# An attention and MLP kernel: the Sync queue's order where the bias table ends, and six tiles' low parts and scalings given to GpSimd in the last attention unit

## The chip, the cores and the metric

One core of one Trainium2 chip. The engines are TensorE (PE; its weight loads are shown as PEld), VectorE (DVE), ScalarE (ACT), GpSimd (POOL) and SyncE (SP), which in this kernel only issues DMAs. The metric is the device time of one execution in microseconds, the lower the better.

## The reference, cut to what matters

```python
B, H, S, D = 4, 8, 576, 64              # hidden of the bias MLP: 32
scores = scale * q @ k.T                 # per batch and head, 576 x 576
x = log1p(|i - j|) / log1p(max(i, 1))    # relative position
bias = relu(x * w1 + b1) @ w2            # one 576 x 576 table per head
attn = softmax(scores + bias)            # with 1e-9 in the divisor
out = attn @ v                           # -> x: 2304 tokens x 512
...
h = x @ w_in                             # 512 -> 2048
g = where(h >= 1, h, where(h <= -1, 0, (h + 1)**2 / 4))
y = g @ w_out                            # 2048 -> 512
```

## The kernel before, in words

The kernel has three stages that overlap at their seams.

**The bias table.** 36 groups `G` of 16 rows of the position table are worked out for all eight heads (ACT and POOL make masks `u`, PE sums them, DVE combines to a tile `y`). Each group's `y` goes to a buffer in HBM by one DMA on the Sync queue (line 332). There are five buffers `bias_d[0..4]`: groups 0 to 7 fill the first, 8 to 15 the second, 16 to 23 the third, 24 to 31 the fourth, and 32 to 35 the last one.

**Attention.** 16 units `n`, one for each of four head pairs `p` and four batches `b` (`n = 4p + b`). In a unit, `k` runs over four blocks of 128 query rows for both heads (`j` = 0, 1) and a fifth block `k = 4` that holds the 64 left rows of both heads (names with `_L`). `scores` (lines 466, 467; 487, 488) makes the scores in PSUM tiles `S` of which there are two, DVE adds the bias and takes the maximum (469, 489), and ACT takes the exponential (476, 495). `transposes` and `shared` (532, 537, 546) bring the result into PSUM tiles `T`, which share four places with the outputs `O` of `values` (570, 572). `split` takes a `T` apart into a high part `hi` and a low part `lo = T - hi`, which PE reads as float32r. There are two ways: either ACT copies `hi` out of PSUM (507) and DVE subtracts (508), or ACT copies the tile to `c` in SBUF (512), POOL (514) or DVE (516) makes `hi`, and POOL subtracts (517). The function `EV` takes the second way for the five blocks `(k, j)` of `POOL` in units 0 to 14, and the first way throughout in unit 15. In the setting `hi='pvvpv'` the blocks (0,1) and (3,0) have their `hi` by POOL and (2,0), (2,1), (3,1) by DVE.

`load_bias(p, k)` brings the bias of one head pair and block to SBUF: three DMAs on the Sync queue for `k < 4` (443 to 445), two for `k = 4` (449). The first pair's five loads are traced ahead of the loop over units, those of pair `p + 1` at fixed places `LB` in the units of pair `p`. `prep(n)` loads a unit's q, k and v; its `part` copies the low and high parts of k to the other half of the partitions by two DMAs on the Sync queue (206, 207).

**The MLP.** `x` (the attention output, stored to HBM as `xT`, line 625) is loaded in quarters `(k, j)` by `split_x` (388, 397), scaled by `scaled` (404: an addition and a multiplication, each 128x384), and taken apart by `high` on ACT (411) and `rest` on POOL (418). The first 768 tokens' eight quarters are loaded and prepared during the attention, at steps given in `XQ`: step `10n + i` is the `i`-th of ten steps of unit `n`, so that the quarter (2,1) is scaled at unit 15's step 1 and (3,1) at its step 5. Weights come in as int64 and are unpacked by `weight` (109, 114 to 119), those of the first two blocks during the attention. The first raw tile of `wout` of the MLP's loop uses the buffer that the quarter (3,1) leaves.

**What sets the order.** The program is traced in the order of the code, and a list scheduler then orders each engine's instructions by readiness and trace order. `keep` (`keep_in_program_order`) pins an instruction behind the one traced before it on its engine. `pool` does so for POOL while `go[0]` is set, which is from the first unit to the start of unit 15. `tc.issue_after(ins)` queues the instructions of its block behind `ins` on the same engine, without a wait for its end. An engine, and the Sync queue too, works through its instructions strictly in order: one that waits holds up all behind it.

```python
for k in range(5):
    e, later = scores(n, k, qkv[n], bias[p])
    ...
    step(2 * k)          # jobs of step 10n + 2k, then the bias loads of LB
    ...
    drain(...)           # transposes and values that lag behind
    exp_()
    step(2 * k + 1)
```

Of the kernel before, what the change touches and what calls it, by code (L numbers as in the profile page):

```python
# [18 lines left out]
B, H, S, D = 4, 8, 576, 64  # L19
# [13 lines left out]
EPS = 1e-9  # L33
RB = 2
LASTP = CFG["lastp"]
XQ = {(0, 0): (39, "raw", 43), (1, 0): (79, "raw", 83), (2, 0): (118, "raw", 123), (3, 0): (137, "bias", 142),
      (0, 1): (125, "x", 136), (1, 1): (131, "raw", 145), (2, 1): (139, "x", 151), (3, 1): (148, "raw", 155)}
WQ = {(0, 0): (49, 53), (0, 1): (59, 63), (1, 0): (89, 93), (1, 1): (99, 103)}
# [9 lines left out]
def attn_cpb_moe_kernel(ctx, tc, qk, vL, cb, win, wout, lw, ident, ii, out):  # L48
    nc = tc.nc
# [26 lines left out]
    ac = loads.enter_context(tc.tile_pool(name="a_const", side="right", bufs=1))  # L76

    qa = [ac.tile([P, 2, QW], F32R, name=f"qa{i}") for i in range(2)]
    wi, wo, last_y = [], [], []
    half_s = wp0.tile([P, 1], F32, name="half_s")  # L80
    nc.gpsimd.memset(half_s, 0.5)
    eps_s = wp0.tile([P, 1], F32, name="eps_s")
# [69 lines left out]
    go = [False]  # L152
# [7 lines left out]
    def keep(ins):  # L160
        tc.keep_in_program_order(ins)

    def pool(ins):
        if KEEP and go[0]:
            tc.keep_in_program_order(ins)
# [53 lines left out]
    with ExitStack() as ph:  # L219
# [101 lines left out]
        def combine(G, A, Bp):  # L321
            right, left, n_ = span(G)
            t = tp.tile([P, S], F32, tag="t", name=f"t{G}")
            y = tp.tile([P, S + 15], F32, tag="y", name=f"y{G}")
            nc.vector.scalar_tensor_tensor(out=t[:, :n_], in0=A[:, :n_], scalar=sg_s[:, G : G + 1], in1=lw8[:, :n_], op0=ALU.mult, op1=ALU.mult)
            for o, c in ((y[:, :left], slice(left, 0, -1)), (y[:, left : left + right], slice(0, right))):
                last_y.append(nc.vector.scalar_tensor_tensor(out=o, in0=Bp[:, c], scalar=s8, in1=t[:, c], op0=ALU.mult, op1=ALU.add))

            r0 = 16 * (G % 8) * H * BW + 1
            dst = bias_d[G // 8][r0 : r0 + 16 * (H * BW + 1)].rearrange("(i w) -> i w", i=16)[:, : H * BW]  # L330
            dst = dst.rearrange("i (h w) -> i h w", h=H)[:, :, : S + 15]
            nc.sync.dma_start(out=dst, in_=y)

        prev = None
        for G in range(NG):
# [38 lines left out]
    def split_x(blk, k, j, home=None):  # L374

        src = xT[k][blk // TB][:, :, TH * j : TH * j + TH].rearrange("(s d) i c -> d s i c", s=2)
        rp, n_ = x_pool() if home is None else (rps[0], home != "raw")
        if n_:
            if home == "bias":
                r = bp.tile([P, 2 * S], F32, tag="bias", name=f"x{blk}_{k}_{j}").rearrange("p (a b) -> p a b", a=3)  # L380
            else:
                r = rp.tile([P, 3, TH], F32, tag="x", name=f"x{blk}_{k}_{j}", bufs=n_)
            r, rr = r[:, 0:2], r[:, 2]
        else:
            r = rp.tile([P, 2 * DM], F32, tag="raw", name=f"x{blk}_{k}_{j}")[:, : 2 * TH].rearrange("p (a b) -> p a b", a=2)
            rr = rp.tile([P, DM], F32, tag="a", name=f"xr{blk}_{k}_{j}")[:, :TH]
        for i in range(2):
            nc.sync.dma_start(out=r[D * i : D * i + D], in_=src[:, :, i])
        c0 = blk + TH * j
        c1 = c0  # L390
        while c1 < c0 + TH:
            t = c1 % S
            e = min(c0 + TH, c1 - t + (512 if t < 512 else S))
            for i in range(2):
                at = 512 * i + t if t < 512 else 1024 + D * i + t - 512
                row = rT[k][c1 // S][at : at + e - c1].unsqueeze(0)
                nc.sync.dma_start(out=rr[D * i : D * i + D, c1 - c0 : e - c0], in_=row.to_broadcast((D, e - c1)))
            c1 = e

        x = r[:, 0]  # L400

        def scaled():
            for op, in1 in ((ALU.add, r[:, 1]), (ALU.mult, rr)):
                a = nc.vector.tensor_tensor(out=x, in0=x, in1=in1, op=op)
                if home:
                    keep(a)

        def high():
            z = (2 * (blk // TB) + j) % 3
            xs[blk, k, j] = [x_tile(z, k, i, f"x{'hl'[i]}{blk}_{k}_{j}") for i in range(2)]  # L410
            a = nc.scalar.copy(xs[blk, k, j][0], x)
            if home:
                keep(a)

        def rest():
            h, l = xs[blk, k, j]
            if home:
                pool(nc.gpsimd.tensor_tensor(out=l, in0=x, in1=h.bitcast(F32), op=ALU.subtract))
            else:
                nc.vector.tensor_tensor(out=l, in0=x, in1=h.bitcast(F32), op=ALU.subtract)  # L420

        if home:
            return scaled, high, rest
        scaled()
        high()
        rest()

    with ExitStack() as ph:
# [8 lines left out]
        def load_bias(p, k):  # L437
            if k < 4:
                if (p, k) in ((1, 1), (2, 3)):
                    t = rps[0].tile([P, 3, TH], F32, tag="x", name=f"bias{p}_{k}", bufs=1).rearrange("p a b -> p (a b)")  # L440
                else:
                    t = bp.tile([P, 2 * S], F32, tag="bias", name=f"bias{p}_{k}")
                nc.sync.dma_start(out=t[:, 0:S], in_=bias_r[k][:, 2 * p, :])
                nc.sync.dma_start(out=t[:, S : S + D], in_=bias_r[k][:, 2 * p + 1, 512:S])
                nc.sync.dma_start(out=t[:, S + D : 2 * S], in_=bias_r[k][:, 2 * p + 1, 0:512])
            else:
                t = bp.tile([P, S], F32, tag="biasL", name=f"biasL{p}", bufs=2)
                for j in range(2):
                    nc.sync.dma_start(out=t[D * j : D * j + D, :], in_=bias_r[4][:, 2 * p + j, :])
            return t  # L450

        def scores(n, k, qkv, bias):
# [65 lines left out]
                pool(r)  # L518

        def EV(n, k, j):  # L520
            return nc.gpsimd if (k, j) in POOL and n < LASTP else None

        def transposes(n, k, es, eT):
            hi, lo = eT
# [55 lines left out]
                c1 = e  # L580

        N = NP * B
        bias = {0: [load_bias(0, k) for k in range(5)]}
        es, eT, sums = {}, {}, {}
        queue, late = [], []

# [51 lines left out]
        for n in range(N):  # L638
            p, b = n // B, n % B
            if n + 2 < N:  # L640
                preps[n + 2] = prep(n + 2)
            es[n] = []
            if n >= LASTP:
                go[0] = False
            for k in range(5):
                e, later = scores(n, k, qkv[n], bias[p])
                es[n].append(e)
                exps = [False]

                def exp_():  # L650
                    if not exps[0]:
                        exps[0] = True
                        for f in later:
                            exps.append(f())

                if CFG["ex"][k] == 0:
                    exp_()
                step(2 * k)
                if p + 1 < NP:
                    for k_ in range(5):  # L660
                        if (b, k) == LB[k_]:
                            bias.setdefault(p + 1, {})[k_] = load_bias(p + 1, k_)

                def tr(n=n, k=k):
                    half = k // 2 if k < 4 else 1
                    if k in (0, 2):
                        w = 256 + D * half
                        eT[n, half] = (
                            (tp0, tp1)[half].tile([P, 9, w], F32R, tag=f"hi{half}", name=f"hi{n}_{half}"),
                            (tp0, tp1)[half].tile([P, 9, w], F32R, tag=f"lo{half}", name=f"lo{n}_{half}"),  # L670
                        )
                    transposes(n, k, es[n], eT[n, half])
                    if k in (1, 4):
                        shared(n, half, es[n], eT[n, half])

                def inv(n=n):
                    nc.vector.reciprocal(out=sums[n], in_=sums[n])

                def rc(n=n):
                    recips(n)  # L680

                if k in (1, 4):
                    def av(n=n, half=0 if k == 1 else 1):
                        values(n, half, es[n], eT[n, half], qkv[n]["v"])
                    queue.append([tr, inv] if k == 4 else [tr])
                    late.append([CFG["lag"][0 if k == 1 else 1], [av] if k == 1 else [av, rc]])
                else:
                    queue.append([tr])
                while late and late[0][0] <= 0:
                    queue.append(late.pop(0)[1])  # L690
                for x in late:
                    x[0] -= 1
                drain(CFG["dr"][k], exp_, CFG["ex"][k])
                exp_()
                step(2 * k + 1)
        queue += [x for _, x in late]
        while queue:
            drain(len(queue) - 1)
# [163 lines left out]
```

## Time and profile before

| | |
|---|---|
| three runs | 756.10, 756.09 and 757.43 us, median 756.1 |
| the profiled execution | 759.95 us, of which the span from the first to the last instruction is 758.2 us |
| PE busy | 712.8 us (94% of the span), mean granted clock 0.993 |
| PEld, DVE, ACT, POOL busy | 631.5, 457.0, 471.6, 414.1 us |

The profiled execution is 3.85 us above the median of the runs. Times in rows are microseconds from the start of the span unless a column says ns. The bias table runs to about 70 us, the attention from there to about 350, the MLP to the end.

### The profile page before, as it was taken

The page shows a single profiled execution, that of the slowest core. Times are in us where ns is not written, and L with a number is a line of the kernel's source. Part 1 is how long each engine was busy: PE and PEld are TensorE (multiplying, and loading weights), DVE is VectorE, ACT ScalarE, POOL GpSimd, SP SyncE. Part 2 cuts the span into 40 slices and gives each one's busy share as a digit, 9 for nine tenths or more (in the row PEclk, how much of TensorE's full clock was granted, in tenths as well). Part 3 has the DMA queues.
Part 4 walks back from the last instruction along what each step waited for, and adds up shares of the span by engine and source line. Part 5 has one row for each costly group of instructions (what it writes and reads, how often), then busy time and mean ns, then how long its engine had stood idle before and what let it go on. Part 6 is the DMA issues. An engine that isn't in the chain of part 4 may idle for free.

```text
span 758.2 us, 13397 instructions
## 1 busy us (share of the span) xinstructions
PE 712.8 (94%) x4688; PEld 631.5 (83%) x4688; DVE 457.0 (60%) x921; ACT 471.6 (62%) x1037; POOL 414.1 (55%) x352
## 2 busy tenths in 40 slices
PE   5777899999999999998999999999999999999997
PEld 2224899998888889988988889898999999999996
DVE  6889778988898898885555642653222252222222
ACT  7997799888888889878997533432222333222222
POOL 8885587888888887853987432222222222222221
PEclk9999999999999999999999999999999999999999
DMA  8889887987997897635575520550000021000002
GB/s 217 249 257 262 223 200 201 272 237 188 262 220 208 199 257 197 168 95 199 194 222 164 157 73 1 149 149 26 1 1 1 0 74 42 0 1 1 1 0 84
DMA packets 58515, 103.35 MB, mean 136 GB/s; under 512 B 12480, under 2 KB 32464, under 8 KB 58448
## 3 DMA queue, kind: packets, MB, share of 16 engines
q1 hardware_dynamic: 56000, 92.44, 42.7%
q0 software_dynamic: 2304, 9.96, 6.5%
q8 instruction: 37, 0.61, 0.3%
q14 instruction: 30, 0.25, 0.1%
q10 hardware_dynamic: 144, 0.09, 0.0%
HBM read 67.38 MB, written 25.12 MB: 122 GB/s over the span
## 4 chain that ended last, share of the span: by engine, by line
PE 63%; DMA 9%; DVE 6%; ACT 6%; issue 4%; POOL 3%; SPq 0%; DVEq 0%; ACTq 0%; POOLq 0%
PE y L743 7%; PE y L744 7%; PE y L742 7%; PE h L721 7%; PE h L723 7%; PE h L722 7%; PE O L570 7%; PE T L532 4%; PE S L466 3%; PE S L467 3%; DMA x<-xT 2%; DMA bias_d<-y 2%; DMA xT<-x 2%; PE O L572 2%; DMA rawo<-in_wout_dram 2%
## 5 line engine op out<-in xcount | busy, mean ns | idle before, releaser
L734 POOL TENSOR_TENSOR gl<-c,gh 128x384 fp32r<-128x384 f32 x96 | 99.9, 1040 | 259.5 <-ACT gh L733 236.3
L731 ACT ACTIVATE c<-c,half_s 128x384 f32<-128x384 f32 x96 | 59.1, 615 | 168.3 <-DVE c L730 168.1
L730 DVE TENSOR_SCALAR c<-h 128x384 f32<-128x384 f32 x96 | 53.2, 555 | 142.2 <-PE h L723 142.2
L721 PE MATMUL h<-xh,wi 128*128 128x384 f32 x352 | 119.7, 340 | 1.8 <-DVE c L732 1.7
L517 POOL TENSOR_TENSOR lo<-c,hi 128x512 fp32r<-128x512 f32 x75 | 101.2, 1365 | 33.9 <-DVE hi L516 31.4
L723 PE MATMUL h<-xh,wi 128*128 128x384 f32 x352 | 118.7, 337 | 0.0
L722 PE MATMUL h<-xl,wi 128*128 128x384 f32 x352 | 118.2, 336 | 0.0
L744 PE MATMUL y<-wo,gl 128*128 128x512 f32 x288 | 114.0, 396 | 0.0
L743 PE MATMUL y<-wo,gh 128*128 128x512 f32 x288 | 113.7, 395 | 0.0
L742 PE MATMUL y<-wo,gh 128*128 128x512 f32 x288 | 111.9, 389 | 0.0
L476 ACT ACTIVATE e<-e,mx 128x576 f32<-128x576 f32 x128 | 100.6, 790 | 11.7 <-DVE mx L469 11.5
L469 DVE CUSTOM_DVE_ANT_0 e<-S,bias 128x576 f32<-128x576 f32 x128 | 94.6, 750 | 15.5 <-PE S L467 12.4
L466 PE MATMUL S<-kh,qa 128*128 128x288 f32 x256 | 78.9, 324 | 9.6 <-DVE mx L469 5.7
L732 DVE TENSOR_TENSOR c<-h,c 128x384 f32<-128x384 f32 x96 | 53.4, 556 | 53.7 <-ACT c L731 53.7
L733 ACT CAST gh<-c 128x384 fp32r<-128x384 f32 x96 | 49.2, 512 | 50.3 <-DVE c L732 48.4
L721 PEld LDWEIGHTS h<-xh,wi 128*128 128x128 f32 x352 | 66.1, 188 | 9.0 <-DVE c L732 5.0
L532 PE MATMUL T<-id_s,e 128*128 128x128 f32 x512 | 71.1, 275 | 2.0 <-DVE hi L516 1.0
L467 PE MATMUL S<-ls,qa 128*128 128x288 f32 x256 | 72.4, 301 | 0.0
L722 PEld LDWEIGHTS h<-xl,wi 128*128 128x128 f32 x352 | 66.1, 188 | 2.5
L723 PEld LDWEIGHTS h<-xh,wi 128*128 128x128 f32 x352 | 66.0, 188 | 0.0
L744 PEld LDWEIGHTS y<-wo,gl 128*128 128x128 f32 x288 | 54.0, 187 | 11.5
L532 PEld LDWEIGHTS T<-id_s,e 128*128 128x128 f32 x512 | 59.2, 142 | 4.6 <-DVE lo L508 1.3
(117 smaller groups left out, 1523.0 us busy)
## 6 DMA issues: line engine op xcount, KB each, us to landing
bias_d<-y SPq DMA_DIRECT2D x36, 295.5 KB, 5.2
qk<-in_qk_dram SPq DMA_DIRECT2D x16, 608.0 KB, 4.5
qa<-in_qk_dram POOLq DMA_DIRECT2D x16, 608.0 KB, 7.2
x<-xT SPq DMA_DIRECT2D x48, 192.0 KB, 3.7
rawo<-in_wout_dram SPq DMA_DIRECT2D x14, 512.0 KB, 3.2
rawi<-in_win_dram SPq DMA_DIRECT2D x14, 512.0 KB, 4.6
v<-in_vL_dram SPq DMA_DIRECT2D x16, 320.0 KB, 3.0
qa<-ls SPq DMA_DIRECT2D x32, 152.0 KB, 5.3
```

The source lines that it names most:

```text
L466: nc.tensor.matmul(ps[:, hf, :HS], qs[:, qc], kh[:, kc : kc + HS], start=True, stop=False)
L467: nc.tensor.matmul(ps[:, hf, :HS], q0[:, qc], kl[:, kc : kc + HS], start=False, stop=True)
L476: lambda ev=ev, j=j: nc.scalar.activation(ev, ev, AF.Exp, bias=mx[:, j : j + 1], scale=-1.0, accum_out=sm[:, 4 * j + k : 4 * j + k + 1])
L517: r = nc.gpsimd.tensor_tensor(out=lo, in0=m, in1=hi.bitcast(F32), op=ALU.subtract)
L532: nc.tensor.transpose(ps[:, tb, :], e[:, c0 : c0 + P], id_s)
L721: nc.tensor.matmul(ps[:, :TH], wh_, xh, start=k == 0, stop=False)
L722: nc.tensor.matmul(ps[:, :TH], wh_, xl, start=False, stop=False)
L723: nc.tensor.matmul(ps[:, :TH], wl_, xh, start=False, stop=k == NK - 1)
L734: nc.gpsimd.tensor_tensor(out=gl, in0=c, in1=gh.bitcast(F32), op=ALU.subtract)
L742: nc.tensor.matmul(y, gh[:, c], wo[f][0], start=f == 0, stop=False)
L743: nc.tensor.matmul(y, gh[:, c], wo[f][1], start=False, stop=False)
L744: nc.tensor.matmul(y, gl[:, c], wo[f][0], start=False, stop=f == NF - 1)
```

## The change

1. The first pair's loads: blocks 0 to 2 stay ahead of the loop; block 3's three DMAs are queued behind the last of the 36 stores of `y`; block 4's two DMAs are traced only at unit 0's block 3.
2. The second pair's bias loads (`p == 1`) are pinned to their traced place on the Sync queue. Those of pairs 0, 2 and 3 are not.
3. In unit 15, the blocks (0,1), (2,0), (2,1) and (3,0) are taken apart by the second way, with the low part by POOL; (3,1) stays with ACT and DVE.
4. The quarters (2,1) and (3,1) of the first 768 tokens are scaled by POOL in place of DVE, pinned in POOL's order.
5. `go[0]` is cleared behind the loop in place of at unit 15's start, so that POOL's instructions in unit 15's steps are pinned too.

```diff
+LATE = ((0, 1), (2, 0), (2, 1), (3, 0))
+XP = ((2, 1), (3, 1))
...
-            nc.sync.dma_start(out=dst, in_=y)
+            stored.append(nc.sync.dma_start(out=dst, in_=y))
...
             for op, in1 in ((ALU.add, r[:, 1]), (ALU.mult, rr)):
+                if home and (k, j) in XP:
+                    pool(nc.gpsimd.tensor_tensor(out=x, in0=x, in1=in1, op=op))
+                    continue
                 a = nc.vector.tensor_tensor(out=x, in0=x, in1=in1, op=op)
...
+            for o, i in parts:
+                x = nc.sync.dma_start(out=o, in_=i)
+                if p == 1:
+                    keep(x)
             return t
...
-            return nc.gpsimd if (k, j) in POOL and n < LASTP else None
+            return nc.gpsimd if (k, j) in POOL and (n < LASTP or (k, j) in LATE) else None
...
-        bias = {0: [load_bias(0, k) for k in range(5)]}
+        bias = {0: {k: load_bias(0, k) for k in range(3)}}
+        with tc.issue_after(stored[-1].ins):
+            bias[0][3] = load_bias(0, 3)
...
-            if n >= LASTP:
-                go[0] = False
             for k in range(5):
+                if (n, k) == (0, 3):
+                    bias[0][4] = load_bias(0, 4)
                 e, later = scores(n, k, qkv[n], bias[p])
...
+        go[0] = False
         queue += [x for _, x in late]
```

## Rows read from the trace of the kernel before

**Rows 1.** The page's first part: busy time, share of the span, instructions.

```profile
PE 712.8 (94%) x4688; PEld 631.5 (83%) x4688; DVE 457.0 (60%) x921; ACT 471.6 (62%) x1037; POOL 414.1 (55%) x352
```

**Rows 2.** Windows at the first seam: length, engines' busy time, clock, DMA share, GB/s.

```profile
66.70:71.60 4.90, 2.84 (x40) 2.08 (x39) 4.90 (x11) 1.90 (x3) 1.76 (x2) 1.00 1.05 251
71.60:75.00 3.40, 2.37 (x17) 2.02 (x17) 3.19 (x8) 2.22 (x6) 1.17 (x1) 1.00 0.84 252
75.00:80.00 5.00, 4.96 (x39) 4.55 (x38) 2.49 (x7) 4.76 (x12) 1.91 (x2) 1.00 0.91 254
80.00:83.00 3.00, 0.96 (x4) 0.99 (x5) 2.31 (x6) 1.17 (x3) 0.00 (x0) 0.86 0.19 48
```

**Rows 3.** Timeline of the Sync queue, first seam: start, time to issue, line, DMA.

```profile
71.63 0.33 SPq L443 DMA_DIRECT2D bias<-bias_d  x1
...
74.04 0.59 SPq L445 DMA_DIRECT2D bias<-bias_d  x1
...
75.31 0.61 SPq L332 DMA_DIRECT2D bias_d<-y  x1
75.96 2.37 SPq L207 DMA_DIRECT2D kh<-kh  x1
...
81.61 1.11 SPq L449 DMA_DIRECT2D biasL<-bias_d  x2
```

**Rows 4.** Waits of the Sync queue from 55 to 90: total, times, longest.

```profile
SPq L443 <- DMA bias_d<-y: 7.1, 3, 4.8
```

**Rows 5.** Timeline of DVE, first seam; in brackets the idle time before.

```profile
80.69 0.76 DVE L469 CUSTOM_DVE_ANT_0 e<-S,bias 128x576 f32<-128x576 f32 x1 [2.56 <-PE S_L L488]
...
85.51 0.76 DVE L489 CUSTOM_DVE_ANT_0 e_L<-S_L,biasL 128x576 f32<-128x576 f32 x1 [1.92 <-DMA biasL<-bias_d]
```

**Rows 6.** Timeline of PE, first seam.

```profile
82.04 0.46 PE L466 MATMUL S<-kh,qa 128*128 128x288 f32 x1 [2.08 <-DMA kh<-kh]
...
91.92 0.63 PE L532 MATMUL T<-id_s,e 128*128 128x128 f32 x4 [1.01 <-DVE hi L516]
```

**Rows 7.** Windows after PE's two long gaps, and the middle of unit 15.

```profile
82.00:86.00 4.00, 3.96 (x20) 3.98 (x21) 2.08 (x5) 1.35 (x3) 1.27 (x1) 0.57 0.68 187
331.10:335.00 3.90, 3.90 (x16) 3.90 (x17) 2.77 (x7) 2.77 (x8) 1.20 (x2) 0.56 0.29 79
332.30:343.00 10.70, 10.70 (x80) 10.64 (x79) 7.91 (x18) 8.15 (x21) 1.01 (x1) 0.88 0.34 89
```

**Rows 8.** Timeline of PE: the longest gap within the attention's steady part.

```profile
216.17 0.41 PE L466 MATMUL S<-kh,qa 128*128 128x288 f32 x1 [1.55 <-DVE mx L469]
```

**Rows 9.** Timeline of DVE around unit 15's start.

```profile
326.58 1.36 DVE L404 TENSOR_TENSOR x<-x 128x384 f32<-128x384 f32 x1
...
328.54 1.65 DVE L404 TENSOR_TENSOR x<-x 128x384 f32<-128x384 f32 x1
...
330.44 0.47 DVE L508 TENSOR_TENSOR lo<-T_s,hi 128x320 fp32r<-128x320 f32 x1
```

**Rows 10.** Timeline of PE there.

```profile
331.07 1.16 PE L570 MATMUL O<-hi,vs 128*128 128x320 f32 x4 [1.59 <-DVE sum L677]
```

**Rows 11.** Timeline of POOL there.

```profile
328.49 2.83 POOL L517 TENSOR_TENSOR lo<-c,hi 128x512 fp32r<-128x512 f32 x2
...
341.76 1.01 POOL L418 TENSOR_TENSOR xl<-x,xh 128x384 fp32r<-128x384 f32 x1 [9.46 <-ACT xh L411]
```

**Rows 12.** POOL's groups by shape from 90 to 318: count, busy us, mean ns.

```profile
L517 POOL TENSOR_TENSOR lo<-c,hi 128x512 fp32r<-128x512 f32 x67 | 90.7, 1370 | 24.7 <-DVE hi L516 22.4
...
L418 POOL TENSOR_TENSOR xh<-x,xh 128x384 fp32r<-128x384 f32 x1 | 1.6, 1640 | 0.0
```

**Rows 13.** Timeline of the Sync queue: the first weight load of the MLP's loop.

```profile
342.80 0.36 SPq L109 DMA_DIRECT2D rawo<-in_wout_dram  x1
```

**Rows 14.** Timeline of ACT in unit 15.

```profile
330.22 0.51 ACT L411 CAST xl<-x 128x384 fp32r<-128x384 f32 x1 [1.00 <-DVE x L404]
...
346.65 0.74 ACT L114 ACTIVATE rawo<-rawo,floor_s 128x512 int32<-128x512 uint16 x1 [0.86 <-DMA rawo<-in_wout_dram]
```

More of the change, by code (lines that the diff above doesn't have):

```diff
@@ L78, in attn_cpb_moe_kernel @@
     qa = [ac.tile([P, 2, QW], F32R, name=f"qa{i}") for i in range(2)]
-    wi, wo, last_y = [], [], []
+    wi, wo, last_y, stored = [], [], [], []
     half_s = wp0.tile([P, 1], F32, name="half_s")
@@ L442, in load_bias @@
                     t = bp.tile([P, 2 * S], F32, tag="bias", name=f"bias{p}_{k}")
-                nc.sync.dma_start(out=t[:, 0:S], in_=bias_r[k][:, 2 * p, :])
-                nc.sync.dma_start(out=t[:, S : S + D], in_=bias_r[k][:, 2 * p + 1, 512:S])
-                nc.sync.dma_start(out=t[:, S + D : 2 * S], in_=bias_r[k][:, 2 * p + 1, 0:512])
+                parts = [
+                    (t[:, 0:S], bias_r[k][:, 2 * p, :]),
+                    (t[:, S : S + D], bias_r[k][:, 2 * p + 1, 512:S]),
+                    (t[:, S + D : 2 * S], bias_r[k][:, 2 * p + 1, 0:512]),
+                ]
             else:
                 t = bp.tile([P, S], F32, tag="biasL", name=f"biasL{p}", bufs=2)
-                for j in range(2):
-                    nc.sync.dma_start(out=t[D * j : D * j + D, :], in_=bias_r[4][:, 2 * p + j, :])
+                parts = [(t[D * j : D * j + D, :], bias_r[4][:, 2 * p + j, :]) for j in range(2)]
+            for o, i in parts:
+                x = nc.sync.dma_start(out=o, in_=i)
+                if p == 1:
+                    keep(x)
             return t
```

## The prediction, made before the changed kernel was run

> **What bounds the kernel now.** I read the page's busy shares first. PE is busy 94% of the span [rows 1], 45 us short of all of it, so that what a change can give lies in PE's gaps and in the stretches in which its clock is low. Next I read PE's timeline for gaps over 1.5 us in the attention. There are three: 2.08 us before unit 1's first scores [rows 6], 1.59 us in unit 15 [rows 10], and 1.55 us in between [rows 8]. The change touches the places of the first two. Each of those is followed by some 4 us in which the granted clock is 0.57 and 0.56, a mix of the two levels, 1.2 and 2.4 GHz [rows 7]: of 4.0 us 43% are lost, 1.7 us, and of 3.9 us 44%, 1.7 us again. Behind the gap of 1.55 us the next scores matmul takes 0.41 us, as against 0.46 us behind that of 2.08 us [rows 6, 8]: there the clock did not fall. What can be had is thus 2.08 + 1.01 + 1.7 us at the first seam (with the gap at 91.92 [rows 6]) and 1.59 + 1.7 us at the second.
>
> Then I read why. **At the first seam** the Sync queue stands 4.8 us for a store of the table to land [rows 4], until 71.63 [rows 3]. The instruction that waits is the first load of bias block 3, and the last stores are behind it; the last store goes out only at 75.31, and the two loads of block 4, which need that store, wait for it until 81.61 [rows 3]. Three things are late from this: DVE stands 2.56 us until 80.69 (the profile names PE, but those scores' bias block 3 is what lands then: the matmul it names works for the block after), DVE stands 1.92 us for block 4 [rows 5], and unit 1's scores wait for the copy of k that was issued at 75.96 [rows 3, 6]. **At the second seam** the output of unit 14's second half needs a place among the four `T` tiles, which the low parts of the left-over rows free; DVE makes these only behind the two scalings of the quarter (2,1), 1.36 and 1.65 us [rows 9].
>
> **The change part by part.** *Block 3 behind the last store.* Removed from the queue's head: the 4.8 us. The last stores no longer wait for it: the last one goes at the latest without the three loads' issue ahead of it, 75.31 - 3 x 0.5 = 73.8, and at the earliest without the wait, 75.31 - 4.8 = 70.5 [rows 3, 4]; I take the middle, 72.1, 3.2 us sooner. What does that give? The DMA engines are not idle while the queue stands: their share is 1.05 there, then 0.84 for 3.4 us and 0.91 for 5.0 us [rows 2]. Stores issued sooner only queue behind what is moving; what can be won by the same bytes in another order is the idle share, 0.16 x 3.4 + 0.09 x 5.0 = 1.0 us. So block 3's last piece and k's copy land about 1.0 us sooner and unit 1 starts at 81.0. Bounds: 0, if bias block 3, now issued behind the stores, lands as late as it does, and 2.08 us.
> *Block 4 later in the trace.* Its source lands with the last store, 3.2 us sooner; then block 4 lands at 85.51 - 3.2 = 82.3, ahead of DVE's need at 85.51 - 1.92 - 1.0 = 82.6 [rows 5]. So DVE's 1.92 us go. The half of k's copy and the next unit's load that stood behind the wait go out too, in the 3 us in which the DMA share is 0.19 [rows 2]. DVE's chain is thus 1.0 + 1.92 = 2.9 us shorter, between 0 and 2.56 + 1.92 = 4.5 us. PE's gap at unit 1 becomes about 1.1 us, less than the one that kept its clock [rows 8], and so PE could follow (its own sum, 1.0 + 1.0 + 1.7, is larger). I take **2.9 us**.
> *The second pair pinned.* Two of its five loads stood directly behind block 4; they go to units 1 and 2 and are needed from unit 4 on. The buffers they take are free or were last read a block before. I cost this at nothing: PE's work of two units hides it. If a load in the way holds up a copy of k, that costs up to its issue, 0.6 us a DMA [rows 3], each time.
> *Low parts by POOL in unit 15.* Four subtractions at 1.37 us [rows 12] are 5.5 us, and two high casts, at no more than a low part's time, up to 2.7 us. ACT copies a tile either way. DVE loses four subtractions and gains two casts. POOL is busy 1.0 of 10.7 us there, DVE 7.9 [rows 7], so both sides lie beside PE's 10.7 busy us.
> *Two quarters by POOL.* DVE loses 3.0 us for (2,1) [rows 9], which stood on the path: the low part that started at 330.44 has 3.0 us less ahead of it and needs only 1.59 us of them for PE's output to follow the scores without the gap [rows 10]; with the gap gone the clock stays, as at 216: 1.59 + 1.7 = 3.3 us by the time the output is complete. On POOL each addition or multiplication is 1.01 us [rows 11] when nothing else is in its way, and up to 1.64 us [rows 12]; I take 1.3, nearer to the contended one as DVE is busy. POOL's order is pinned: unit 14's last low parts end at 331.3 [rows 11], the quarter's two operations at 333.9; then one cast, one low part, the quarter's own low part (1.0), the second quarter's 2.6, two low parts, 2.7, and its low part, 1.0. From 331.3 that is 2.6 + 1.4 + 1.4 + 1.0 + 2.6 + 2.7 + 1.0 = 12.7 us, hence 344.0 without waits, and 342.8 with the four operations at 1.01. The same operation ended at 342.8 before, and on it hangs the first weight load, at 342.80 [rows 13], for which ACT stood 0.86 us at 346.65 [rows 14] with the casts of unit 15's last block behind it. So ACT meets this wait earlier than before, and what PE gained is partly given back there. Bounds for the seam: a gain of 3.3 us if PE's work of the MLP fills in, and a loss as in the fourth rival. I take half, **1.5 us**: the load hardly moves, but PE has MLP matmuls to do meanwhile.
>
> The sum: 759.95 - 2.9 - 1.5 = 755.55 us for the profiled execution. It lay 3.85 us above the runs' median; 4.4 us off the median of 756.1 is **751.7 us**.
>
> **The rivals.** *First, the DMA engines decide.* Their share of 1.05 while the queue stands [rows 2] says that the stores would only wait elsewhere; against it stands the share of 0.19 after 80. Then the first seam gives nothing and the second 1.5: 754.6 us. The Trainium skill's page DMA: Bandwidth & Descriptors, section Issuing engines are not separate DMA queues, states that all DMAs end on the same 16 engines and that what is saved at issue is usually small beside the transfer; by that rule it is this case. The trace agrees in part, with 1.05 in one stretch and 0.19 in another.
> *Second, unit 15's gain is given back* at the weights' wait in full [rows 13, 14]: 756.1 - 2.9 = 753.2 us.
> *Third, both seams pay in full*: 4.5 + 3.3 us, 748.3 us. PE's sum speaks for it, the DMA shares against.
> *Fourth, on the other side: POOL sets unit 15.* ACT's cast of the quarter (2,1) stood at 330.22 [rows 14]; it now needs POOL's multiplication, at 331.3 + 2 x 1.64 = 334.6. If that cast stands in ACT's queue ahead of the left-over block's cast, ACT and with it the exponentials of unit 15 are 4.4 us late, and POOL's chain ends near 346. The gap of 1.59 us stays and grows. Lost: 4.4 us, plus the cast's 0.5; with the first seam's 2.9 us this gives 756.1 + 4.9 - 2.9 = 758.1 us. It decides once ACT's wait there exceeds 2.9 us. For it speaks that POOL's two low parts there already run at 1.4 us each [rows 11]; against, that the scheduler sees POOL's queue and can let other ACT work pass. The Trainium skill's Perfetto Trace Analysis, section Optimizing Scalar/DVE Operations, warns that GpSimd and DVE share an SBUF read port, so that offloading between them might not help; by that rule the time would go this way. The trace has DVE's scalings at 1.36 and 1.65 us beside a busy POOL, which bears on it.
> *Fifth, no change*: the scheduler reorders the queue such that each wait finds a new place; 756.1 us.
>
> **How the numbers follow.** A measurement of this kernel can tell about 0.2%, 1.5 us, from no change. Chances: the forecast 0.42 (its own range 749.5 to 754), the first rival 0.17, the second 0.14, the third 0.09, the fourth 0.13, the fifth 0.05. The first rival's time is at the edge, so half of it counts as faster, and a part of the second's spread does not: faster 0.42 + 0.08 + 0.11 + 0.09 = 0.70, less 0.03 for the spread of the forecast itself, 0.67; slower 0.13, with 0.01 of the fifth, 0.14; same 0.19. The range runs from 747.8 to 757.4: it leaves out most of the fourth rival (0.12) and the far side of the third (0.05).
>
> **What would show each step.** Right: the last store before 73 us and no wait of 4 us on the Sync queue between 66 and 72; DVE's waits at the scores of block 3 and block 4 below 1.6 and near 0; unit 1's first scores at about 81 with a granted clock near 1.00 in the 4 us after; unit 15's gap below 0.5 us with no low clock behind it; POOL's low part of (3,1) at or before 343. Wrong: block 3's load used later than 80.7 (the DMAs decide), unit 1 no earlier; ACT waiting for POOL in unit 15 by more than 1 us, or for the first raw weight by more than 2; gaps of PE in units 2 to 14 that add up to more than before.

## The result, and the profile after

The changed kernel takes 764.65 us (median of 7 runs, 761.98 to 768.69), the kernel before 757.43 us (7 runs, 754.53 to 762.27): a ratio of 1.0090, interval 1.0062 to 1.0119. It is slower by about 7 us, where 4.4 us less had been forecast. Its profiled execution took 765.94 us.

The page's first part and the windows at the first seam, after (columns as in [rows 1, 2]):

```profile
PE 715.7 (94%) x4688; PEld 633.8 (83%) x4688; DVE 455.8 (60%) x915; ACT 473.1 (62%) x1037; POOL 422.1 (55%) x362
```

```profile
66.70:71.60 4.90, 3.12 (x41) 2.40 (x40) 4.90 (x13) 1.93 (x2) 2.15 (x2) 1.00 0.98 241
71.60:75.00 3.40, 2.37 (x18) 2.12 (x17) 3.18 (x7) 2.11 (x7) 0.77 (x1) 1.00 0.90 251
75.00:80.00 5.00, 4.56 (x36) 4.13 (x34) 2.10 (x7) 4.88 (x13) 1.90 (x2) 1.00 0.90 188
80.00:83.00 3.00, 1.65 (x10) 1.44 (x11) 2.47 (x6) 0.99 (x4) 0.00 (x0) 0.88 0.86 256
81.30:85.30 4.00, 3.95 (x21) 3.74 (x22) 3.89 (x8) 1.57 (x4) 1.61 (x2) 0.63 0.34 117
```

POOL is busy 8 us longer, no other engine by more than 3. PE's extra 2.9 us are not more instructions (x4688 as before). At the seam the DMA share is as high while the last stores go out as it was before [rows 2], and what was left idle at 80 to 83 is now filled. Next the Sync queue, DVE and PE there, one fence each:

```profile
70.95 0.49 SPq L208 DMA_DIRECT2D qa<-ls  x1
71.53 0.55 SPq L334 DMA_DIRECT2D bias_d<-y  x1
72.18 1.65 SPq L457 DMA_DIRECT2D bias<-bias_d  x3
75.77 3.35 SPq L457 DMA_DIRECT2D biasL<-bias_d  x2
```

```profile
80.53 0.76 DVE L479 CUSTOM_DVE_ANT_0 e<-S,bias 128x576 f32<-128x576 f32 x1 [2.78 <-DMA bias<-bias_d]
...
83.53 0.76 DVE L499 CUSTOM_DVE_ANT_0 e_L<-S_L,biasL 128x576 f32<-128x576 f32 x1
```

```profile
81.35 0.40 PE L476 MATMUL S<-kh,qa 128*128 128x288 f32 x1 [1.79 <-DVE mx L479]
```

The last store goes out at 71.53 in place of 75.31 [rows 3], and DVE's wait for block 4 is gone [rows 5]. But block 3, now behind the stores, is used at 80.53, as against 80.69 [rows 5], and unit 1 starts only 0.7 us sooner [rows 6]; PE's gap is still 1.79 us, and in the 4 us behind it the granted clock is 0.63, as against 0.57 [rows 7].

In unit 15, ACT, POOL, DVE and PE, after:

```profile
332.36 0.51 ACT L416 CAST xl<-x 128x384 fp32r<-128x384 f32 x1 [3.52 <-POOL x L407]
332.78 0.37 ACT L517 CAST hi<-T_L 128x256 fp32r<-128x256 f32 x1
...
334.28 0.60 ACT L522 COPY c<-T 128x512 f32<-128x512 f32 x1
```

```profile
327.75 2.53 POOL L527 TENSOR_TENSOR lo<-c,hi 128x512 fp32r<-128x512 f32 x2
330.23 2.09 POOL L407 TENSOR_TENSOR x<-x 128x384 f32<-128x384 f32 x2
334.94 0.61 POOL L524 CAST hi<-c 128x512 fp32r<-128x512 f32 x1 [2.62 <-ACT c L522]
...
344.30 1.30 POOL L423 TENSOR_TENSOR xl<-x,xh 128x384 fp32r<-128x384 f32 x1
```

```profile
333.18 0.42 DVE L518 TENSOR_TENSOR lo<-T_L,hi 128x256 fp32r<-128x256 f32 x1 [3.27 <-ACT hi L517]
```

```profile
333.65 0.56 PE L580 MATMUL O<-hi,vs 128*128 128x320 f32 x2 [2.57 <-DVE lo L518]
```

The cast of the quarter (2,1) waits 3.52 us for POOL, where it had waited 1.00 for DVE [rows 14]. Behind it in ACT's queue stand the left-over block's cast (DVE waits 3.27 us for it, and PE's output for DVE: 2.57 us in place of 1.59 [rows 10]) and the copy `c`, for which POOL itself now stands 2.62 us. POOL makes ACT late, and ACT then POOL, so that the quarter (3,1) is ready at 345.6, not 342.8 [rows 11].

Where the 5.8 us between the two spans (764.0 and 758.2) come from is read off PE's timeline at three marks: unit 15's first scores, and the first low-part output matmul (`y<-wo,gl`) of hidden blocks 1 and 9, counted from 0, of the MLP's first 768 tokens. **A** is the time from the first mark to the second, **B** the eight hidden blocks from the second to the third, 336 matmuls in every run. After less before: -0.4 us up to unit 15, +1.75 in A (46.51 and 44.76), **+4.75 in B** (73.59 and 68.84), -0.3 behind. The largest term is at a place that the change does not edit. Eight blocks in which PE waits for nothing take 66.99 us (in e15 to e19 below). PE's waits from 350 to 450, before and then after (total, times, longest):

```profile
PE h L721 <- DVE c L732: 1.7, 3, 1.2
...
PE h L734 <- DVE c L745: 6.0, 8, 1.4
```

### The profile page after: what moved, and what is told of

Read it like the earlier page. It is cut to its first block, busy times and chain, and to the rows that moved or that the text cites. A ratio compares the mean times of both kernels' runs of the same rounds, so it can differ in the third digit from the quotient of the medians.

```text
span 764.0 us, 13408 instructions
## 1 busy us (share of the span) xinstructions
PE 715.7 (94%) x4688; PEld 633.8 (83%) x4688; DVE 455.8 (60%) x915; ACT 473.1 (62%) x1037; POOL 422.1 (55%) x362
## 5 line engine op out<-in xcount | busy, mean ns | idle before, releaser
L744 ACT ACTIVATE c<-c,half_s 128x384 f32<-128x384 f32 x96 | 59.2, 617 | 164.0 <-DVE c L743 164.0
L743 DVE TENSOR_SCALAR c<-h 128x384 f32<-128x384 f32 x96 | 53.2, 554 | 144.8 <-PE h L736 143.7
L527 POOL TENSOR_TENSOR lo<-c,hi 128x512 fp32r<-128x512 f32 x79 | 105.4, 1349 | 34.8 <-DVE hi L526 26.7
L745 DVE TENSOR_TENSOR c<-h,c 128x384 f32<-128x384 f32 x96 | 53.4, 556 | 52.3 <-ACT c L744 52.2
L542 PE MATMUL T<-id_s,e 128*128 128x128 f32 x512 | 72.7, 279 | 1.0 <-DVE lo L518 0.8
```

The costliest lines, as they stand in the source:

```text
L527: r = nc.gpsimd.tensor_tensor(out=lo, in0=m, in1=hi.bitcast(F32), op=ALU.subtract)
L542: nc.tensor.transpose(ps[:, tb, :], e[:, c0 : c0 + P], id_s)
```

## The experiments

Two theories stood at the start: that the seam's part gives nothing and all of the loss is unit 15's (ACT waiting for POOL), or that the Sync queue's new order costs something itself, by pinned loads in the way of others. Each run was timed in five rounds, beside the kernel before on the same chip. The ratio is to that kernel; A and B are those of the one profiled execution. The edits are shown against the changed kernel; e7, e14 and e16 are the same edits on the kernel before. Kernels with the same order on PE, DVE, ACT and POOL agree in A within 0.7 us (before and e1, after and e2, e5 and e11), in B within some 2 us.

| run | ratio [95%] | A | B |
|---|---|---|---|
| before (profiled) | | 44.76 | 68.84 |
| after | 1.0090 [1.0062, 1.0119] | 46.51 | 73.59 |
| e1 seam only | 1.0002 [0.9975, 1.0029] | 44.06 | 70.23 |
| e2 unit 15 only | 1.0063 [1.0033, 1.0092] | 46.18 | 71.55 |
| e3 low parts only | 1.0022 [0.9992, 1.0052] | 44.11 | 71.61 |
| e4 quarters only | 1.0005 [0.9977, 1.0034] | 43.15 | 71.33 |
| e5 after, a cast later | 0.9991 [0.9970, 1.0012] | 41.46 | 71.11 |
| e11 e2, a cast later | 1.0017 [0.9996, 1.0038] | 41.12 | 72.03 |
| e12 e2, both casts later | 0.9980 [0.9951, 1.0009] | 40.22 | 72.29 |
| e6 after, casts by DVE | 1.0143 [1.0113, 1.0174] | 46.66 | 77.76 |
| e7 before, casts by DVE | 1.0142 [1.0108, 1.0176] | 44.42 | 79.49 |
| e8 e3, casts by DVE | 1.0104 [1.0071, 1.0137] | 44.73 | 79.48 |
| e13 after, no shift | 1.0156 [1.0131, 1.0182] | 45.12 | 76.65 |
| e14 before, no shift | 1.0153 [1.0123, 1.0183] | 43.13 | 79.19 |
| e15 after, pinned | 1.0014 [0.9985, 1.0043] | 43.91 | 66.99 |
| e16 before, pinned | 0.9974 [0.9951, 0.9998] | 41.95 | 66.99 |
| e17 e12, pinned | 0.9930 [0.9907, 0.9953] | 39.32 | 66.99 |
| e18 e17 and the seam | 0.9929 [0.9906, 0.9951] | 39.08 | 66.99 |
| e19 e16 and the seam | 0.9958 [0.9933, 0.9984] | 42.45 | 66.99 |

**The change in its parts (e1 to e4).** In e1 the Sync queue's part stands alone:

```diff
-LATE = ((0, 1), (2, 0), (2, 1), (3, 0))
-XP = ((2, 1), (3, 1))
+LATE = ()
+XP = ()
...
+            if n >= LASTP:
+                go[0] = False
```

> The first seam's part alone (blocks 3 and 4 of the first pair, the second pair pinned); unit 15 as before. Theory (unit 15's part costs the time, in the unit itself and in the MLP's first block): within 1.5 us of before, from 2 us faster to 1 slower, and the first block of the MLP loses nothing. Rival (the Sync queue's new order costs it, by way of everything that is scheduled behind it): slower by 4 us or more, with the MLP's first block longer by 4.

In e2 the seam's part is undone:

```diff
-                if p == 1:
-                    keep(x)
...
-        bias = {0: {k: load_bias(0, k) for k in range(3)}}
-        with tc.issue_after(stored[-1].ins):
-            bias[0][3] = load_bias(0, 3)
+        bias = {0: {k: load_bias(0, k) for k in range(5)}}
...
-                if (n, k) == (0, 3):
-                    bias[0][4] = load_bias(0, 4)
```

> Unit 15's part alone (four low parts, two quarters, pins to the end); the Sync queue as before. Theory: slower by 5 to 8 us, 1 to 2 of them by the end of the attention, the rest between the MLP's blocks 3 and 9 of the hidden layer. Rival: slower by 2 us at most.

e3 is e2 with `XP = ()`, e4 is e2 with `LATE = ()`.

> The four low parts by GpSimd in unit 15 and the pins to the end, with the two quarters' scalings back on VectorE; the Sync queue as before. Theory (the scalings are what ScalarE waits for): within 1.5 us of before at the end of the attention, no wait of ScalarE over 1.2 us at the cast of the quarter (2,1). Rival (the low parts make the last unit late): 1 us or more late at the end of the attention. For the MLP's first block no theory has a number yet: 0 if it follows from the late attention, 4 to 5 us if any new order of the weights' start brings it.

> The two quarters' scalings by GpSimd and the pins to the end, with the low parts as before; the Sync queue as before. Theory: ScalarE stands 3 to 4 us at the cast of the quarter (2,1), unit 14's last outputs are 2 us or more late, the attention ends 1 to 2 us late; in all slower by 1.5 to 7 us. Rival: no wait there, within 1.5 us.

The seam's part alone is worth nothing, 1.0002. Its instructions stand in the same order as before on every engine but the Sync queue, so that nothing else differs. Its interval still allows 1.9 us of gain; the other pairs with and without it narrow that at the end of this section. Unit 15's part alone costs 0.63% (4.8 us, a little less than the 5 to 8 expected). Neither half of it costs that much alone: 0.22% and 0.05%, each with no change in its interval. With the quarters alone (e4) ACT's wait is there in full, and PE's gap too:

```profile
331.25 0.51 ACT L416 CAST xl<-x 128x384 fp32r<-128x384 f32 x1 [3.56 <-POOL x L407]
...
332.55 1.43 PE L578 MATMUL O<-hi,vs 128*128 128x320 f32 x4 [2.60 <-DVE lo L516]
```

But A is no longer than before, 43.15 us, and the kernel 0.05% slower, where 1.5 to 7 us had been expected: a miss. No low part of unit 15 on POOL needs ACT's copy there, so the delay does not come back through POOL. I read this as a loop that only both halves together close; the times of e2, e3 and e4 fit it, but their intervals overlap.

**The cast moved (e5, e11, e12).** In e5, on the whole change, ACT's cast of (2,1) and its low part are traced two steps later:

```diff
-                    plan(T1 + i, f)
+                    plan(T1 + (i + 2 if i and (k, j) == (2, 1) else i), f)
```

> The changed kernel with ScalarE's cast of the quarter (2,1) and its low part two steps later in the trace. Theory (the cast waits for GpSimd's multiplication and holds up ScalarE's queue): the wait of 3.5 us is gone, the gap of TensorE before unit 14's last outputs falls from 2.57 us to under 1, and the start of the MLP's first down projection comes 1.5 to 3 us sooner after unit 15's first scores than in the changed kernel (38.1 us). Rival (GpSimd's own lateness sets unit 15): the wait moves to the low parts and that distance stays above 37. In all 1.5 to 3 us faster than the changed kernel, if the MLP's first block is as it was there.

ACT's timeline of e5:

```profile
327.46 0.36 ACT L517 CAST hi<-T_L 128x256 fp32r<-128x256 f32 x1
...
331.04 0.51 ACT L416 CAST xl<-x 128x384 fp32r<-128x384 f32 x1
...
335.37 0.51 ACT L416 CAST xh<-x 128x384 fp32r<-128x384 f32 x1 [2.05 <-POOL x L407]
```

The left-over block's cast now goes ahead, the quarter's cast finds its operand ready, and A falls from 46.51 to 41.46 us, 3.3 us below the kernel before. The whole change then measures 0.9991. That ACT's wait, and what came back of it, made A longer is thus shown; the fall of 5.05 us is more than the 1.75 that A had grown, and more than the 1.5 to 3 expected, so other gaps went with it. e11 is the same edit on e2; e12 moves (3,1)'s cast by two steps as well.

> Unit 15's part with the cast of the quarter (2,1) two steps later, and the Sync queue's order of before. PE, DVE, ACT and POOL have the same order as in the run with the whole change and the later cast. Theory (the seam's part gives nothing and its new order costs up to 1.3 us by unit 15's first scores, 321.2 against 319.9 on average): no wait of 3.5 us on ScalarE, first scores of unit 15 to first down projection 33 to 34 us, first hidden blocks 79 to 80 us, 0.997 to 1.000 of the time before, 0 to 1.3 us below the run with the whole change and the later cast (0.9991). Rival (the seam's part does give something): 1.002 or more.

> The same, with the casts of both quarters on ScalarE, (2,1) and (3,1), two steps later. Theory: ScalarE's other wait in unit 15, 2.05 us at the cast of (3,1), goes as well, and unit 15 is 0 to 2 us shorter than with one cast moved. Rival: (3,1)'s low part now ends later on POOL, the first raw weight tile waits for its buffer, and the MLP's first blocks get longer by as much: no gain, 79 us there become 81.

A is 41.12 and 40.22 us. But B stays at 71 to 72 us, and the totals at that of the kernel before. e11's 1.0017 lies above the 0.997 to 1.000 expected, and next to the rival's 1.002: by this pair the seam's part would give 2 us.

**Why B is long: two misses (e6 to e8, e13, e14).** My first theory was that ACT is full while weights are unpacked (23 of 25 us in the kernel before). e6, e7 and e8 give the weights' high cast in `weight` to DVE, in after, before and e3:

```diff
-        nc.scalar.copy(h, t.bitcast(F32))
+        nc.vector.tensor_copy(h, t.bitcast(F32))
```

> The changed kernel with the high part of every weight tile of the MLP's loop cast by VectorE in place of ScalarE (28 casts of 0.52 us). Theory (ScalarE is the bound of the MLP's first block while the weights are unpacked, and what it loses in waits TensorE loses): nine hidden blocks take 75.4 to 77 us in place of 82.0, the whole is 4 to 6 us faster than the changed kernel, at most 2 us slower than before. Rival (the raw loads' landing or the order of the instructions sets it): 80 us or more.

> The kernel before with the same casts moved to VectorE. Theory: nine hidden blocks take 75.4 to 76.5 us in place of 77.2, the whole is 0.5 to 2 us faster than before. Rival: no change, or slower by what VectorE's longer queue adds.

> The four low parts alone (the quarters and the Sync queue as before) with the same casts moved to VectorE. Theory: unit 15 as in the run of the low parts alone (1.5 us shorter to the attention's last output than before), nine hidden blocks 75.4 to 77 us, the whole 1.5 to 3.5 us faster than before. Rival: the first block stays at 79 to 80 us, the whole 1 us or more slower than before.

All three got slower. The groups from 360 to 410: e7's join and cast on DVE, before's join on DVE, before's cast on ACT:

```profile
L116 DVE SCALAR_TENSOR_TENSOR ai<-ai,rawi 128x512 int32<-128x512 int32 x11 | 12.4, 1124 | 0.5 <-ACT ai L115 0.5
...
L118 DVE CAST wi<-ai 128x512 fp32r<-128x512 f32 x11 | 11.6, 1052 | 0.1
```

```profile
L116 DVE SCALAR_TENSOR_TENSOR ai<-ai,rawi 128x512 int32<-128x512 int32 x12 | 11.2, 935 | 8.9 <-ACT ai L115 8.9
```

```profile
L118 ACT CAST wi<-ai 128x512 fp32r<-128x512 f32 x12 | 7.4, 618 | 1.3 <-DVE ai L116 1.3
```

The cast takes 1052 ns on DVE where it took 618 on ACT, and the join beside it grows from 935 to 1124 ns: DVE became full (45.7 of 50 us), and these runs say nothing about ACT. (The expectation of e6 put a cast at 0.52 us; on ACT it takes 0.62.) So e13 and e14 take work from ACT and give it to no one; they leave out the low three bits of the weights:

```diff
-        nc.scalar.activation(lo, raw.bitcast(U16).rearrange("p a (b c) -> p a b c", c=2)[:, :, 0, 1], AF.Identity, scale=2.0**-13, bias=floor_s)
...
-        nc.vector.scalar_tensor_tensor(out=t, in0=t, scalar=3, in1=lo, op0=ALU.logical_shift_left, op1=ALU.bitwise_or)
+        nc.vector.scalar_tensor_tensor(out=t, in0=t, scalar=3, in1=lo, op0=ALU.logical_shift_left, op1=ALU.bitwise_and)
```

> The whole change, with ScalarE's first operation of each weight tile in the MLP's loop left out (the low three bits of the weights are left out). Theory (ScalarE's fill is what makes the MLP's first hidden blocks long, and the changed kernel's order meets it harder): nine blocks, 82.0 us with the change and 77.2 to 78.6 us without, fall to 75.4 to 77 us in both, and the difference between the two kernels to that of unit 15, 1.3 to 2 us. Rival (the waits come from transfers, or from POOL, or DVE's new order): 79 us or more stay with the change, and the difference between the kernels stays near 7 us.

> The kernel before with the same operation left out (the low three bits of the weights are left out). Theory: nine blocks in 75.4 to 77 us, 1 to 3 us below the kernel before in all. Rival: 77 to 79 us, as before.

With less to do, both take some 12 us more than the kernel before, e13 thus 5 us more than the changed kernel, and B is 77 to 79 us. The window from 360 to 400, before and then in e14:

```profile
360.00:400.00 40.00, 40.00 (x203) 36.34 (x202) 24.02 (x36) 37.23 (x68) 34.89 (x26) 1.00 0.65 210
...
360.00:400.00 40.00, 34.87 (x164) 30.33 (x164) 28.88 (x31) 27.79 (x50) 34.90 (x26) 0.96 0.65 210
```

In e14 ACT is busy 27.8 of 40 us, and PE still waits; before, with ACT busy 37.2 us, PE waited for nothing. The theory that a full ACT sets B fell.

But DVE has grown from 24.0 to 28.9 us with fewer instructions. Its joins for `wi` from 360 to 440, in after, e14 and e15 (before: 935 ns, above):

```profile
L118 DVE SCALAR_TENSOR_TENSOR ai<-ai,rawi 128x512 int32<-128x512 int32 x12 | 13.8, 1148 | 10.2 <-ACT ai L117 10.2
...
L115 DVE SCALAR_TENSOR_TENSOR ai<-ai,rawi 128x512 int32<-128x512 int32 x12 | 15.0, 1258 | 6.0 <-ACT ai L114 6.0
...
L118 DVE SCALAR_TENSOR_TENSOR ai<-ai,rawi 128x512 int32<-128x512 int32 x10 | 7.3, 726 | 17.4 <-ACT ai L117 17.4
```

By the timelines of all the profiles, a join that overlaps with no instruction of POOL takes 0.67 to 0.70 us; of those that overlap, some take over 1 us, the longest 1.77. The joins of B take 0.85 us on average before, 0.97 in after, 1.22 and 1.17 in e13 and e14. So the order of the queues need not be all that makes e13 and e14 long: their joins meet POOL's work more. How much of their B that makes, no run separates. It is not what made B long everywhere: in e3, e5 and e12 the joins take 0.85 to 0.87 us, as before, and B is 71 to 72 us.

**The order, pinned (e15 to e17).** What B waits for stands in after's timeline, DVE, ACT, POOL and PE together, ahead of PE's gap at 392.46 (rows between them left out):

```profile
388.57 0.69 DVE L118 SCALAR_TENSOR_TENSOR ao<-ao,rawo 128x512 int32<-128x512 int32 x1 [2.47 <-ACT ao L117]
...
389.18 0.55 DVE L743 TENSOR_SCALAR c<-h 128x384 f32<-128x384 f32 x1
...
389.37 0.62 ACT L120 CAST wo<-ao 128x512 fp32r<-128x512 f32 x1
...
389.89 0.66 ACT L117 ACTIVATE ai<-rawi 128x512 f32<-128x512 f32 x1
...
390.45 0.75 ACT L116 ACTIVATE rawi<-rawi,floor_s 128x512 int32<-128x512 uint16 x1
390.58 1.36 DVE L118 SCALAR_TENSOR_TENSOR ai<-ai,rawi 128x512 int32<-128x512 int32 x1 [0.85 <-ACT ai L117]
...
391.10 0.60 ACT L744 ACTIVATE c<-c,half_s 128x384 f32<-128x384 f32 x1
...
391.86 0.55 DVE L745 TENSOR_TENSOR c<-h,c 128x384 f32<-128x384 f32 x1
...
392.46 0.45 PE L734 MATMUL h<-xh,wi 128*128 128x384 f32 x1 [0.87 <-DVE c L745]
```

A hidden block's PSUM tile comes free by DVE's clamp (L743), ACT's square (L744) and DVE's maximum (L745). The clamp at 389.18 stood behind a weight's join that waited 2.47 us for ACT; the square, ready to go at 389.7, stood behind three operations on weights until 391.10; the maximum stood behind another join. Unpacking runs ahead of its need there: ACT does 31 of its operations in hidden blocks 3 to 5 (30 in the kernel before), where two weight tiles a block, three operations each, ask for 18. So the next runs pin unpacking (ACT and DVE) behind the hidden block that it is traced after, with all its work in place (the activation of `lo` likewise):

```diff
-        nc.scalar.activation(a, hi.bitcast(F32), AF.Prelu, scale=2.0**-112, alpha=-(2.0**32))
-        nc.vector.scalar_tensor_tensor(out=t, in0=t, scalar=3, in1=lo, op0=ALU.logical_shift_left, op1=ALU.bitwise_or)
+        keep(nc.scalar.activation(a, hi.bitcast(F32), AF.Prelu, scale=2.0**-112, alpha=-(2.0**32)))
+        keep(nc.vector.scalar_tensor_tensor(out=t, in0=t, scalar=3, in1=lo, op0=ALU.logical_shift_left, op1=ALU.bitwise_or))
...
-        nc.scalar.copy(h, t.bitcast(F32))
+        keep(nc.scalar.copy(h, t.bitcast(F32)))
```

> The whole change, and the weights' unpacking in the MLP's loop pinned on ScalarE and VectorE behind the hidden block's operations that are traced ahead of it. Nothing is left out. Theory (the static order, in which unpacking runs four and more blocks ahead of its use and stands ahead of clamps and squares, makes the first blocks long): nine hidden blocks take 75.4 to 77 us in place of 82.0, and the whole 757 to 760 us, 0.999 to 1.003 of before. Rival (throughput of an engine or the transfers of raw weights): 79 us or more stay.

> The kernel before with the same pins. Theory: nine blocks in 75.4 to 77 us in place of 77.2 to 78.6, 1 to 3 us below the kernel before, and the changed kernel with the same pins is 1 to 3 us above this one (unit 15's wait alone). Rival: longer than before, since pinned unpacking comes too late for the first blocks.

> Unit 15's part with both casts two steps later, the Sync queue's order of before, and the same pins. Theory: the nine blocks fall from 80.7 to 75.4 to 77 us, so 3 to 5 us below the version without pins (0.998 of before): 0.992 to 0.995 of before. Rival: no change, 0.997 to 0.999.

B is 66.99 us in all three, PE's own time. Windows of e15, then e17:

```profile
366.00:390.00 24.00, 24.00 (x123) 21.86 (x122) 10.47 (x19) 17.04 (x30) 13.85 (x12) 1.00 0.38 132
```

```profile
400.00:425.00 25.00, 25.00 (x127) 22.64 (x127) 10.31 (x18) 17.00 (x31) 13.68 (x13) 1.00 0.36 127
```

ACT is busy 17 of 25 us and PE all the time: the static order made B long, in the kernel before as well. The pins change several things with it, which these runs do not separate: what stands ahead of a clamp or a square, how much unpacking falls into B (50 operations of ACT in place of 63 before and 64 in after; all 84 are still done), and DVE's joins, which take 0.71 us on average. After less before, both pinned, is 0.40% (1.0014 and 0.9974, some 3 us), of which A shows 43.91 - 41.95 = 1.96 us and B nothing. e17 is faster than both kernels, 0.9930. The pins give some of it back: from the third mark to the end takes 323.6 to 323.7 us in e15 to e19, as against 322.0 before. In e15, e16 and e17 it is one wait of PE, 60 us behind the third mark, where the next 768 tokens begin; the kernel before has none there. In e15:

```profile
491.38 0.44 PE L734 MATMUL h<-xh,wi 128*128 128x384 f32 x1 [1.73 <-DVE c L745]
```

Why that maximum comes late there stays open.

**The seam once more (e18, e19)**, with B's spread gone: the Sync queue's part added to e17 and to e16.

> Both casts later and the pins, as in the run that gave 0.993 of before, now with the Sync queue's part of the change as well; the order on all other engines is the same as there. Theory (the first seam gives nothing): 0.992 to 0.995. The prediction's term (2.9 us at the first seam): 0.988 to 0.990. Rival (the new order costs about 1 us): 0.994 to 0.997.

> The kernel before with the pins, which gave 0.9974, now with the Sync queue's part of the change. Theory (nothing): 0.996 to 0.999. The prediction's term: 0.993 to 0.995. Rival (costs 1 us): 0.998 to 1.001.

0.9929 beside 0.9930, and 0.9958 beside 0.9974, just below the 0.996 to 0.999 expected. With e1 beside before, after beside e2, and e5 beside e11 there are five pairs of equal order on PE, DVE, ACT and POOL, with and without the Sync queue's part: +0.02, +0.27, -0.26, -0.01 and -0.16%, on average -0.03%. The forecast's 2.9 us would be -0.38%. No gain, and no loss that these runs can tell.

## Why the prediction was wrong

**The first seam (forecast 2.9 us, measured 0).** On the queue three of the signs that I had named came: no wait of 4.8 us, the last store before 73, DVE's wait for block 4 gone. Behind it they did not: DVE's wait for block 3 was 2.78 us, not below 1.6, PE's gap 1.79, not about 1.1, and the clock behind it 0.63, not near 1.00. What failed is "block 3's last piece and k's copy land about 1.0 us sooner", for block 3, and, with it, "DVE's chain is thus 1.0 + 1.92 = 2.9 us shorter". Block 3's use moved by 0.16 us, the bound that I had given as 0, and from there unit 1's start is set. The 1.92 us of block 4 were no longer in the way of anything that PE needed: PE now waits 1.79 us for DVE's maximum of block 3. The share of 1.05 while the queue stood [rows 2] spoke for this: the first rival's reading. The rule that I weighed there, of the Trainium skill's page DMA: Bandwidth & Descriptors, section Issuing engines are not separate DMA queues (what is saved at issue is small beside the transfer; the page says it of issuing from several engines), fits these two profiles: the last store is issued 3.8 us sooner, and the use of block 3, loaded behind it, starts 0.16 us sooner. My sign for the clock was weak as well: the first scores matmul takes 0.40 us behind this gap and 0.41 behind that of 1.55 us [rows 8], but here the clock fell, and there it stayed at 1.00 (216.2 to 220.2).

A second error is in the yardstick, and it goes deeper: the gap that I meant to close is mostly not there. Of the 11 profiles with the old queue order, PE waits 2.08 us ahead of unit 1's first scores in before and 2.06 in e14, and at most 0.64 in the other nine. Unit 1 starts at 80.77 us on average in these 11 and at 80.79 in the eight with the new order; from unit 0's first scores to unit 2's it is 31.28 and 31.27 us. The profiled execution of before lay 3.85 us above the median, and I took 4.4 us off the median for gaps seen in that execution. Its unit 15 started at 322.59 us. The ten other kernels here whose engines have the same order up to that point (e2 to e4, e7, e8, e11, e12, e14, e16, e17) started it at 318.46 to 323.91, 320.08 on average. So 2.5 us of the 3.85 lay ahead of unit 15, and what I meant to win at the first seam was not there in most executions. The eight profiles with the new queue order started it at 319.77 to 324.88, 321.22 on average: no gain either.

**Unit 15 (forecast -1.5 us, measured about +2 us in A).** The failed step is "with the gap gone the clock stays". The gap did not go, and in the 4 us behind it the clock was 0.66 (333.6 to 337.6). The durations were sized well: POOL's two scalings took 2.09 us (1.3 each assumed), and a low part 1.27. What failed is the assumption that the cast on ACT would not stand ahead of the left-over block's cast. This was the fourth rival, with 0.13; I priced ACT's wait at 4.4 us, it was 3.52. I gave the scheduler credit for letting other work pass. The sum also added up POOL's chain as if it had no waits; it had 2.62 us for ACT's copy, a loop that no part of my sum held. With the cast two steps later the gain is there: A is 3.3 us below the kernel before in e5, the same 3.3 us that I had as the upper bound, but that the two agree is luck, since part of it comes from other gaps. As to the Trainium skill's warning on GpSimd and DVE (Perfetto Trace Analysis, Optimizing Scalar/DVE Operations): the time went its way, but in unit 15 the loss came by the queues. POOL's scalings of (2,1) ran at 1.05 us each, near the 1.01 us of [rows 11], but DVE did nothing in those 2.09 us, so that these rows cannot test the warning. The MLP's blocks fit it: DVE's joins take 0.67 to 0.70 us without POOL's work beside them and up to 1.77 us with it. That the shared port is the reason, no run shows.

**The MLP's first blocks (not in the forecast, +4.75 us in the profiles).** I costed the change up to the first raw weight's load and no further. But a new order in unit 15 gives the list scheduler other ready times, and it writes another order for everything behind. Clamps and squares had stood behind unpacking already before (68.84 us against 66.99), and by count they do so no more often in the changed kernel: of the 54 clamps, squares and maxima of hidden blocks 1 to 9, 38 stand directly behind unpacking before, 37 after. But they come later: from its last matmul to the end of its maximum a hidden tile holds its PSUM place 5.1 us on average before, 6.0 after, 2.8 with the pins. That the static order is the cause is shown by the pins, with no work removed: B is equal to 0.01 us in both kernels. By which way it works, a queue that stands or joins that meet POOL's work, stays open. How much of the 4.75 us belongs to the change and how much to the single execution is less sure. Kernels with equal orders differ there by some 2 us: 73.59 in after, 71.55 in e2, and 68.84 in before, 70.23 in e1. Mean against mean that is about 3 us. With the 2 us of A this makes e2's 4.8; after's 6.8 us (0.90%) lies above it, within both intervals.

## What to carry to other kernels

Before work is moved to another engine, look in each queue at what stands behind the first instruction that will consume it, and follow the delay until it comes back to the engine that caused it: here moving one cast by two steps gave back all that the whole change had cost. Where a list scheduler writes the order, an edit reprices everything traced behind it; compare the order of the stages that follow, and pin work that is not urgent behind the work that the bound engine waits for. And look for a gap in other executions of the same order before it goes into a sum that starts from the median.

## What the runs showed of the hardware that was not expected

Taking an operation away from ACT (e14) made the kernel before 1.5% slower. The weights' cast took 1052 ns on DVE (e7, with POOL busy 39.8 of 50 us) and 618 ns on ACT. One and the same join on DVE took 0.67 to 0.70 us where it overlapped with no instruction of POOL, and up to 1.77 us where it did. Two profiled executions of kernels that have one order on every engine up to unit 15 lay up to 5.5 us apart at that point (318.46 and 323.91 us).
